# Score banks in units of three, one ring for the probabilities, and numerators divided in halves

## The chip, the cores and the metric

The kernel runs on one core of one Trainium2 chip. The metric is the device time of one execution in microseconds (us). A core has a matrix engine (PE, which writes only to the accumulator memory PSUM), a vector engine (DVE), an activation engine (ACT), a general engine (POOL) and a queue engine (SP) that issues transfers. PSUM has 8 banks per partition, and a bank holds 512 fp32 values. Each engine works through its own instructions in program order and waits for the others through semaphores.

## The reference, cut to what matters

For x of 2048 tokens by 640 (32 heads of 20), the output is `g * A + (1 - g) * B`, with a gate g per token. A is a linear attention with softmax features. B, the part that the change touches, splits the tokens into four segments of 512 and runs, for each head,

```
logits = q @ k.T * scale + mask          # causal within the segment
a_dot  = softmax(logits) @ v
a_mem  = (phi(q) @ M) / (phi(q) @ z + 1e-6)
o      = sig(beta) * a_mem + (1 - sig(beta)) * a_dot
M     += phi(k).T @ v ;  z += sum(phi(k))    # carried to the next segment
```

with `phi(t) = t + 1 if t > 0 else exp(t)`. All heads' o, joined, are multiplied by `wo`.

## The kernel before, in words

The kernel first does all of A and the projections that B's first segment needs (to about 146 us of the profile). Everything the change touches is the second half, "stage B" (L580 to L902), whose order on every engine is the program's order (`manual_schedule`).

Work goes by steps: a step is one segment s and one group g of four heads, so there are 4 x 8 = 32. Keys and queries stand transposed, four heads of 32 rows each. For a step the scores (keys by queries) of key chunk c are computed only for queries from chunk c on: 512, 384, 256 and 128 columns. A bank holds, for one head i, chunk 0 of a step, or chunks 1 and 3 of a step, or chunk 2 of two steps. So two steps fill 20 banks.

`emit_scores` (L613) is a unit of work: two banks, for the heads i0 and i0 + 1. PE makes their scores with matmuls of 32 rows, placed on the row group of their head (L618), and ACT makes exp of both banks into a tile PT (L622). After the second unit of a kind, POOL zeroes the triangles above the diagonal (L630). A pair of steps is ten units, n = 0 to 9.

Between the units PE is given other work, by hand:

- `emit_pv` (L666) multiplies probabilities with v: 40 matmuls of 21 columns for a step (L674), into `nda`. For step a of a pair it is cut into query chunks 0 to 2 (24 matmuls, after unit 9) and chunk 3 (16 matmuls, after unit 0 of the next pair). For step b these come after the units 3 and 4.
- `emit_mem` (L677) adds the memory's part, 4 matmuls (L681), and the next memory's increment, 4 matmuls (L686).
- `emit_epi` (L690) divides, on DVE: reciprocal (L695), weight (L697), one product over both numerators of 640 columns (L707; in segment 0 one of 320, L703), and the memory's increment (L712). POOL adds the halves into oB (L709).
- A half item is a projection of 128 tokens for the next segment, 320 columns wide: 5 matmuls (L505), then a DVE cast (L515). An output half is 5 matmuls (last segment's rows, in segment 0) or 10 (L743), then a DVE cast (L749). `gaps_of` (L790) says after which unit each comes; in most gaps there is one.
- `emit_eq` (L718) and `emit_phiq` (L723) make phi(q) with one ACT and two DVE instructions per step. `turn_keys` (L759) does the same for keys of the next segment (L524, L764, L528).

The PSUM banks of stage B: `bst` two buffers of two banks (scores), `bnd` one buffer of two banks (`nda`), `bps` two buffers of one bank (projections and outputs). A buffer is free for PE when everything that read its last tile is done (`reuse_waits="tile"`).

The tail (L843 to L902) finishes the last two steps, transposes oB on PE with copies on ACT (L858, L859), multiplies with wo (L863), adds the part of A on DVE (L870) and sends the rows out.

Of the kernel before, what the change touches and what calls it, by code (L numbers as in the profile page):

```python
# [15 lines left out]
def kernel(  # L16
# [563 lines left out]
    with ExitStack() as bctx:  # L580
# [7 lines left out]
        bpt = bctx.enter_context(tc.tile_pool(name="bpt", bufs=2))  # L588
# [4 lines left out]
        bps = bctx.enter_context(tc.tile_pool(name="bps", bufs=2, space=bass.MemoryType.PSUM,  # L593
                                              reuse_waits="tile"))
        oBs, ogs = {}, {}
        GP = 4 * (DH + 1)

        class Step:
            def __init__(self, k):
                self.s, self.g = divmod(k, G)  # L600
                self.PT = {}
                self.phiq = None
                if self.g == 0:
                    oBs[self.s] = bw.tile([P, 4, D], BF16, name="oB")
                    og = Eqf[:, 2 * G * L + 2 * L + (self.s % 2) * L:2 * G * L + 2 * L + (self.s % 2 + 1) * L]
                    og = og.bitcast(F32).rearrange("p (n j h) -> p n j h", n=2, j=4)
                    om = omgS[:, 4 * self.s:4 * self.s + 4, None].to_broadcast([P, 4, H])
                    nc.gpsimd.tensor_tensor(out=og[:, 0], in0=om, in1=omgh_b[:, None, :].to_broadcast([P, 4, H]),
                                            op=ALU.mult)
                    nc.gpsimd.tensor_copy(out=og[:, 1], in_=om)  # L610
                    ogs[self.s] = og

        def emit_scores(parts, i0, PT):  # L613
            ps = bst.tile([P, 2, L], F32, name="st_ps")
            for step, c, o in parts:
                kT, qT = (t[step.s % 2][:, step.g] for t in (kTs, qTs))
                for i in (i0, i0 + 1):
                    nc.tensor.matmul(ps[:, i - i0, o:o + L - c * P],  # L618
                                     lhsT=kT[32 * i:32 * i + 32, c * P:(c + 1) * P],
                                     rhs=qT[32 * i:32 * i + 32, c * P:L],  # L620
                                     start=True, stop=True, tile_position=(32 * i, 0))
            nc.scalar.activation(out=PT[:, i0:i0 + 2], in_=ps, func=ACT.Exp, scale=SCALE_B)  # L622

        def triangles(PT, at):
            if at == (0, 2):
                parts = [(PT.rearrange("p i (n t) -> p (i n) t", t=256)[:, :, 0:P], 8)]
            else:
                parts = [(PT[:, :, n * P:(n + 1) * P], 4) for n in at]
            for v, n in parts:
                nc.gpsimd.affine_select(out=v, in_=v, pattern=[[0, n], [1, P]], compare_op=ALU.is_ge,  # L630
                                        fill=0.0, base=0, channel_multiplier=-1)

        def units(a, b):
            out = []
            for st in (a, b):
                for n, parts in enumerate((((st, 0, 0),), ((st, 1, 0), (st, 3, 384)))):
                    PT = bpt.tile([P, 4, L], BF16, name=f"PT{n}")
                    for i0 in (0, 2):
                        def unit(parts=parts, i0=i0, PT=PT, n=n):
                            emit_scores(parts, i0, PT)  # L640
                            if i0 == 2:
                                triangles(PT, (0, 3) if n else (0,))
                        out.append(unit)
                    st.PT[0 if n == 0 else 1] = PT
                if st is a:
                    PT = bpt.tile([P, 4, L], BF16, name="PT2")
                    for i0 in (0, 2):
                        def unit(i0=i0, PT=PT):
                            emit_scores(((a, 2, 0), (b, 2, 256)), i0, PT)
                            if i0 == 2:  # L650
                                triangles(PT, (0, 2))
                        out.append(unit)
                    a.PT[2], b.PT[2] = (PT, 0), (PT, 256)
            return out

        def block(st, c):
            if c == 0:
                return st.PT[0]
            if c == 1:
                return st.PT[1][:, :, 0:384]  # L660
            if c == 3:
                return st.PT[1][:, :, 384:512]
            PT, o = st.PT[2]
            return PT[:, :, o:o + 256]

        def emit_pv(st, js):  # L666
            if js[0] == 0:
                st.nda = bnd.tile([P, 2, 512], F32, name="nda")
            nd = st.nda[:, 0, 0:4 * GP].rearrange("p (j i e) -> p j i e", j=4, i=4)
            vB = vBs[st.s % 2]  # L670
            for j in js:
                for i in range(4):
                    for c in range(j + 1):
                        nc.tensor.matmul(nd[:, j, i], lhsT=block(st, c)[:, i, (j - c) * P:(j - c + 1) * P],  # L674
                                         rhs=vB[:, c, 4 * st.g + i, :], start=(c == 0), stop=(c == j))

        def emit_mem(st):  # L677
            g = st.g
            if st.s > 0:
                for j in range(4):  # L680
                    nc.tensor.matmul(st.nda[:, 1, j * GP:(j + 1) * GP], lhsT=st.phiq[:, j * P:(j + 1) * P],  # L681
                                     rhs=Mbd[:, g].rearrange("p i e -> p (i e)"), start=True, stop=True)
            if st.s < NSEG - 1:
                Mz = st.nda[:, 1, 4 * GP:5 * GP].rearrange("p (i e) -> p i e", i=4)
                for c in range(4):
                    nc.tensor.matmul(Mz, lhsT=phiks[st.s % 2][:, c, 4 * g:4 * g + 4, :],  # L686
                                     rhs=vBs[st.s % 2][:, c, 4 * g:4 * g + 4, :],
                                     start=(c == 0), stop=(c == 3))

        def emit_epi(st):  # L690
            s, g = st.s, st.g
            n = 2 if s > 0 else 1
            ndv = st.nda[:, 0:n, 0:4 * GP].rearrange("p n (ji e) -> p n ji e", e=DH + 1)
            rec = bw.tile([P, 2, 16], F32, name="rec")
            nc.vector.reciprocal(out=rec[:, 0:n], in_=ndv[:, :, :, DH])  # L695
            recv = rec[:, 0:n].rearrange("p n (j i) -> p n j i", j=4)
            nc.vector.tensor_tensor(out=recv, in0=recv,  # L697
                                    in1=ogs[s][:, 0:n, :, 4 * g:4 * g + 4],
                                    op=ALU.mult)
            rb = rec[:, 0:n, :, None].to_broadcast([P, n, 16, DH])  # L700
            oview = oBs[s][:, :, g * 80:(g + 1) * 80].rearrange("p j (i d) -> p j i d", d=DH)
            if n == 1:
                nc.vector.tensor_tensor(out=oview, in0=ndv[:, 0, :, 0:DH].rearrange("p (j i) d -> p j i d", j=4),  # L703
                                        in1=rb[:, 0].rearrange("p (j i) d -> p j i d", j=4), op=ALU.mult)
            else:
                td = bw.tile([P, 2, 16, DH], F32, name="td")
                nc.vector.tensor_tensor(out=td, in0=ndv[:, :, :, 0:DH], in1=rb, op=ALU.mult)  # L707
                tdv = td.rearrange("p n (j i) d -> p n j i d", j=4)
                nc.gpsimd.tensor_tensor(out=oview, in0=tdv[:, 0], in1=tdv[:, 1], op=ALU.add)  # L709
            if s < NSEG - 1:  # L710
                mtmp = bw.tile([P, 4, DH + 1], F32, name="mtmp")
                nc.vector.tensor_tensor(  # L712
                    out=mtmp, in0=st.nda[:, 1, 4 * GP:5 * GP].rearrange("p (i e) -> p i e", i=4),
                    in1=CM[:, g, :, :], op=ALU.mult)
# [3 lines left out]
        def emit_eq(st):  # L718
            eq = Eqf[:, 2 * G * L + (st.g % 2) * L:2 * G * L + (st.g % 2 + 1) * L]
            nc.scalar.activation(out=eq, in_=qTs[st.s % 2][:, st.g], func=ACT.Exp)  # L720
            return eq

        def emit_phiq(st, eq):  # L723
            nc.vector.tensor_scalar_min(out=eq, in0=eq, scalar1=1.0)
            st.phiq = bw.tile([P, L], BF16, name="phiq", bufs=3)
            nc.vector.scalar_tensor_tensor(out=st.phiq, in0=qTs[st.s % 2][:, st.g], scalar=0.0, in1=eq,
                                           op0=ALU.max, op1=ALU.add)
# [6 lines left out]
        oTs, rows = {}, {}  # L734

        def emit_out_half(ch, half):
# [13 lines left out]
            if half == 1 and not early:  # L750
                nc.sync.dma_start(out=out2[ch * P:(ch + 1) * P, :], in_=rows[ch])

        clock = [0]
        due = {}

        def defer(n, fn):
            due.setdefault(clock[0] + n, []).append(fn)

        def turn_keys(sc):  # L759
            emit_turn("k", sc, kTs[(sc // 4) % 2])  # L760
            if sc < NCH - 4:
                def feature():
                    ek = emit_ek(bw, sc)
                    nc.vector.tensor_scalar_min(out=ek, in0=ek, scalar1=1.0)  # L764
                    defer(2, lambda: emit_phik(sc, ek))
                defer(2, feature)
# [10 lines left out]
        def half_items(s, order):  # L777
            return [half_item(part, 4 * s + c, half) for part, c in order for half in range(2)]

        CHUNKED = [(part, c) for c in range(4) for part in "kqv"]  # L780
        FIRST_SEG = [(part, c) for c in range(4) for part in "kq"]
# [151 lines left out]
```

## Time and profile before

| what | value |
|---|---|
| median of 3 runs | 367.07 us (363.47 to 370.16) |
| the profiled execution's own time | 369.4 us |
| its span, first to last instruction | 367.3 us |
| mean granted PE clock | 0.963 |
| PE busy | 337.1 us (92%) |
| ACT busy | 265.1 us (72%) |
| DVE busy | 231.0 us (63%) |
| POOL busy | 205.3 us (56%) |
| first to last exp of stage B | 146.0 to 349.0 us |

The profile counts an instruction as busy from its start to its end. Matmuls are pipelined, so that PE's rows overlap; what an instruction costs PE is read from its start to the next one's start. The granted clock is the share of full speed at which PE was allowed to run.

### The profile page before, as it was taken

What the parts mean: (1) busy time and instruction counts of PE and PEld (TensorE: products, weight loads), DVE (VectorE), ACT (ScalarE), POOL (GpSimd) and SP (SyncE); (2) the same over time, 40 slices, a digit from 0 to 9 for tenths busy, and PEclk for the clock granted to TensorE, in tenths of its full rate; (3) what the DMA queues carried; (4) which work ended last, traced back from release to release, by engine and by line L of the source; (5) the groups of instructions that cost most, each with busy time, mean ns of one, the idle gap of its engine ahead of it and who ended that gap; (6) DMA issues with size and microseconds to landing.
All of it is one profiled execution on the core that took longest, in us unless ns stands there. A gap on an engine that the chain in (4) does not pass through costs nothing.

```text
span 367.3 us, 9701 instructions
## 1 busy us (share of the span) xinstructions
PE 337.1 (92%) x4025; PEld 223.7 (61%) x4025; DVE 231.0 (63%) x469; ACT 265.1 (72%) x342; POOL 205.3 (56%) x283
## 2 busy tenths in 40 slices
PE   7999999899789998898989989889999999999974
PEld 6788888854367775455444455555565655665652
DVE  3466976598778895454353576777667665656533
ACT  4888978058444556987797788778889788898911
POOL 8177598103168778464454466576567456545530
PEclk9999999999899999999995799999999999999969
DMA  8749988980037778422311334213432351130002
GB/s 240 229 88 184 107 109 111 222 297 0 2 16 130 117 112 130 76 42 48 59 31 30 75 39 77 48 33 51 90 59 43 64 85 36 40 74 36 20 20 72
DMA packets 68806, 30.68 MB, mean 84 GB/s; under 512 B 54554, under 2 KB 68762, under 8 KB 68762
## 3 DMA queue, kind: packets, MB, share of 16 engines
q1 hardware_dynamic: 67898, 29.24, 42.0%
q10 hardware_dynamic: 864, 0.82, 0.8%
q8 instruction: 31, 0.51, 0.6%
q14 instruction: 13, 0.11, 0.1%
HBM read 9.21 MB, written 2.62 MB: 32 GB/s over the span
## 4 chain that ended last, share of the span: by engine, by line
PE 65%; ACT 12%; DVE 10%; DMA 6%; issue 5%; POOL 1%; SPq 1%; ACTq 0%; DVEq 0%
PE proj L505 13%; PE st_ps L618 10%; PE o_ps L743 9%; ACT PT L622 9%; PE nda L674 8%; PE pk L213 6%; PE pv L213 6%; PE pq L264 5%; DVE tt L453 2%; DMA Z<-Z 2%; DMA x_nat<-in_A_x_dram 2%; PE num L409 2%; DVE zz L250 2%; DVE rr L431 1%; DMA Z<-EkSn 1%
## 5 line engine op out<-in xcount | busy, mean ns | idle before, releaser
L622 ACT ACTIVATE PT<-st_ps 128x1024 bf16<-128x1024 f32 x160 | 155.6, 1028 | 33.7 <-PE st_ps L618 22.4
L630 POOL TENSOR_SCALAR_AFFINE_SELECT PT<-PT 128x512 bf16<-128x512 bf16 (+1 forms) x112 | 79.4, 726 | 51.0 <-ACT PT L622 50.9
L505 PEld LDWEIGHTS <-xT 128*128 128x128 bf16 x480 | 42.1, 100 | 26.5 <-issue 13.3
L225 POOL TENSOR_TENSOR EkSn<-Ek,krec 128x1280 bf16<-128x1280 bf16 x16 | 37.6, 2360 | 17.6 <-DVE krec L224 15.8
L674 PEld LDWEIGHTS <-PT 128*128 128x128 bf16 x1280 | 36.9, 96 | 15.4 <-issue 12.9
L674 PE MATMUL nda<-vB,PT 128*128 128x21 bf16 x1280 | 42.4, 174 | 1.9 <-DVE td L707 1.7
L213 PEld LDWEIGHTS <-xT 128*128 128x128 bf16 x320 | 35.3, 113 | 7.0 <-ACT xT L191 0.2
L618 PE MATMUL st_ps<-Z 32*128 32x512 bf16 (+3 forms) x256 | 30.2, 302 | 7.6 <-ACT PT L622 5.7
L709 POOL TENSOR_TENSOR oB<-td 128x320 bf16<-128x320 f32 x24 | 20.7, 862 | 23.8 <-DVE td L707 23.8
L618 PE MATMUL st_ps<-Eq 32*128 32x512 bf16 (+3 forms) x256 | 30.1, 314 | 2.9 <-ACT PT L622 2.5
L515 DVE CAST Z<-proj 128x320 bf16<-128x320 f32 x48 | 23.3, 486 | 14.9 <-PE proj L505 14.3
L221 DVE TENSOR_REDUCE ksum<-Ek 128x64 f32<-128x1280 bf16 x16 | 23.6, 1478 | 12.4 <-ACT Ek L217 12.4
L743 PE MATMUL o_ps<-WkA,oTA 128*128 128x320 bf16 x160 | 27.5, 303 | 3.0 <-DVE Z L515 3.0
L269 ACT ACTIVATE Eq<-pq 128x1024 bf16<-128x1024 f32 x20 | 19.4, 1021 | 14.7 <-PE pq L264 14.7
L453 DVE TENSOR_TENSOR tt<-num,rr 128x640 f32<-128x640 f32 x32 | 25.2, 814 | 6.7 <-PE num L409 5.2
L505 PE MATMUL proj<-WqB,xT 128*128 128x320 bf16 x160 | 29.2, 316 | 0.0
L554 POOL TENSOR_TENSOR oA<-tt 128x640 bf16<-128x640 f32 x16 | 24.7, 1548 | 7.6 <-DVE tt L453 6.8
L505 PE MATMUL proj<-WkB,xT 128*128 128x320 bf16 x160 | 28.5, 311 | 0.0
L505 PE MATMUL proj<-WvB,xT 128*128 128x320 bf16 x160 | 27.5, 305 | 0.0
L217 ACT ACTIVATE Ek<-pk 128x640 bf16<-128x640 f32 x32 | 20.8, 701 | 7.7 <-PE pk L213 5.3
L409 PEld LDWEIGHTS <-Eq 128*128 128x128 bf16 x384 | 20.3, 97 | 9.3 <-issue 6.9
L213 PE MATMUL pv<-WvA,xT 128*128 128x321 bf16 x160 | 24.6, 300 | 0.0
(135 smaller groups left out, 540.1 us busy)
## 6 DMA issues: line engine op xcount, KB each, us to landing
Z<-EkSn SPq DMA_DIRECT2D x32, 160.0 KB, 4.9
x_nat<-in_A_x_dram SPq DMA_DIRECT2D x8, 320.0 KB, 6.4
out_dram<-orow SPq DMA_DIRECT2D x12, 160.0 KB, 1.8
WvA<-in_A_wqkv_dram SPq DMA_DIRECT2D x2, 400.0 KB, 6.1
wnat_q<-in_A_wqkv_dram SPq DMA_DIRECT2D x1, 800.0 KB
WkB<-in_B_wk_dram SPq DMA_DIRECT2D x1, 800.0 KB, 7.2
WqB<-in_B_wq_dram SPq DMA_DIRECT2D x1, 800.0 KB, 9.0
WvB<-in_B_wv_dram SPq DMA_DIRECT2D x1, 800.0 KB, 10.6
```

What stands on the lines that cost most here:

```text
L213: nc.tensor.matmul(ps[:, bk, 0:n], lhsT=xTk[:, c, sc // 4, sc % 4], rhs=rhs, start=(c == 0), stop=(c == KC - 1))
L221: nc.vector.tensor_reduce(out=ksum, in_=Ek.rearrange("p s (h f) -> p (s h) f", f=DH), axis=AX.X, op=ALU.add)
L225: nc.gpsimd.tensor_tensor(out=EkSn[:, sc].rearrange("p s (h f) -> p (s h) f", f=DH), in0=Ek.rearrange("p s (h f) -> p (s h) f", f=DH), in1 ...
L409: nc.tensor.matmul(ps(bk, lo, hi), lhsT=Eqs[qb, j][:, sgn, qc * P:(qc + 1) * P], rhs=kvx[:, sgn, j, lo - h0:hi - h0, :].rearrange("p h e - ...
L453: nc.vector.tensor_tensor(out=tt[:, sgn].rearrange("p (b h) d -> p b h d", b=2), in0=ps, in1=csb, op=ALU.mult)
L505: nc.tensor.matmul(ps, lhsT=xT[:, cc, sc * P:(sc + 1) * P], rhs=W[:, cc, half * 320:(half + 1) * 320], start=(cc == 0), stop=(cc == KC - 1))
L554: nc.gpsimd.tensor_tensor(out=oA.rearrange("p (h d) -> p h d", d=DH), in0=tt[:, 0], in1=tt[:, 1], op=ALU.add)
L618: nc.tensor.matmul(ps[:, i - i0, o:o + L - c * P], lhsT=kT[32 * i:32 * i + 32, c * P:(c + 1) * P], rhs=qT[32 * i:32 * i + 32, c * P:L], st ...
L622: nc.scalar.activation(out=PT[:, i0:i0 + 2], in_=ps, func=ACT.Exp, scale=SCALE_B)
L630: nc.gpsimd.affine_select(out=v, in_=v, pattern=[[0, n], [1, P]], compare_op=ALU.is_ge, fill=0.0, base=0, channel_multiplier=-1)
L674: nc.tensor.matmul(nd[:, j, i], lhsT=block(st, c)[:, i, (j - c) * P:(j - c + 1) * P], rhs=vB[:, c, 4 * st.g + i, :], start=(c == 0), stop= ...
L743: nc.tensor.matmul(ps, lhsT=oT[:, k5], rhs=W[:, k5, hs], start=(n == 0 and k5 == 0), stop=(n == len(srcs) - 1 and k5 == KC - 1))
```

## The change

- **Units of three banks.** The 20 banks of a pair of steps become one stream over all steps, 320 banks, cut into 107 units of three (the last has two). PE fills the three banks of a unit, ACT makes exp of all three with one instruction. A unit may run across two kinds of bank. `bst` has two buffers of three banks.
- **The ring.** The probabilities go to one tile of 24 banks, used in turn. The triangles of four banks are zeroed when the fourth is done, as before.
- **Half steps.** `emit_pv` takes a step in two halves of two query chunks: h = 0 has 12 matmuls, h = 1 has 28, each with 2 matmuls of the memory (and h = 1 with the increment). Each half uses one bank, X; `bnd` has one buffer of one bank. Each half is divided right behind: reciprocal, weight, product of 2 x 160 columns.
- **One bank for projections and outputs**: `bps` has one buffer.
- **Dealing.** Items are laid out over a segment and dealt to the units so that the planned cost (0.7 for a half item, 1.38 for an output half, 0.45 and 1.05 for the halves of a step) is spread evenly. In a unit come: the scores, the first item if any, the half step if any, further items. Half steps of step k come in the first and second unit after its last bank (k even) or the second and third (k odd). phi(q) is moved to the end of a unit's work.
- **Outputs**: segments 1, 2, 3 take 4, 4 and 16 output halves (before 3, 5 and 16).
- **Tail.** The first 512 columns of oB are transposed by four transfers in place of PE and ACT. The part of A enters by a matmul with the identity, and the results leave PSUM by copies on DVE and ACT in turn, each followed by a transfer of its half rows.

```diff
-        bpt = bctx.enter_context(tc.tile_pool(name="bpt", bufs=2))
+        bpt = bctx.enter_context(tc.tile_pool(name="bpt", bufs=1))
...
-        bps = bctx.enter_context(tc.tile_pool(name="bps", bufs=2, space=bass.MemoryType.PSUM,
+        bps = bctx.enter_context(tc.tile_pool(name="bps", bufs=1, space=bass.MemoryType.PSUM,
...
+        UB = 3
+        RING = 24
+        ring = bpt.tile([P, RING, L], BF16, name="PT")
...
+        def emit_unit(u):
+            banks = list(range(UB * u, min(UB * u + UB, 10 * NST)))
+            ps = bst.tile([P, UB, L], F32, name="st_ps")
+            todo = [(n, bank(b)) for n, b in enumerate(banks)]
+            for turn in range(2):
+                for n, (kind, i, parts) in todo:
+                    if turn < len(parts):
+                        st, c, o = parts[turn]
+                        kT, qT = (t[st.s % 2][:, st.g] for t in (kTs, qTs))
+                        nc.tensor.matmul(ps[:, n, o:o + L - c * P], ...
+            r0 = banks[0] % RING
+            nc.scalar.activation(out=ring[:, r0:r0 + len(banks)], in_=ps[:, 0:len(banks)],
+                                 func=ACT.Exp, scale=SCALE_B)
...
+        def emit_pv(st, h):
+            s, g = st.s, st.g
+            X = bnd.tile([P, 512], F32, name="X")
+            W2 = 2 * GP
+            nd = X[:, 0:W2].rearrange("p (j i e) -> p j i e", j=2, i=4)
...
+            rec = bw.tile([P, 2, 2, 4], F32, name="rec")
+            nc.vector.reciprocal(out=rec[:, 0:n], in_=v[:, :, :, :, DH])
+            nc.vector.tensor_tensor(out=rec[:, 0:n], in0=rec[:, 0:n],
+                                    in1=ogs[s][:, 0:n, 2 * h:2 * h + 2, 4 * g:4 * g + 4], op=ALU.mult)
...
+                nc.vector.tensor_tensor(out=st.td[:, :, 8 * h:8 * h + 8], in0=v8, in1=rb, op=ALU.mult)
...
+            late = 2 if k % 2 else 1
+            for h in range(2):
+                pv_at.setdefault(min(st_done + late + h, NU + 3), []).append((k, h))
...
+            load = {u: sum(1.05 if h else 0.45 for _, h in pv_at.get(u, ())) for u in us}
+            items = items_of(s)
+            total = sum(load.values()) + sum(c for _, c, _ in items)
+            cum = 0.0
+            for n, u in enumerate(us):
+                cum += load[u]
+                while items and (cum + items[0][1] / 2 <= total * (n + 1) / len(us) or u == us[-1]):
+                    plan[u].append(items[0][2])
+                    cum += items.pop(0)[1]
...
+        for u in range(NU):
+            now[0] = u
+            emit_unit(u)
+            work = plan[u]
+            for fn in work[0:1]:
+                fn()
+            for k, h in pv_at.get(u, ()):
+                emit_pv(step(k), h)
+            for fn in work[1:]:
+                fn()
+            for k in eq_at.get(u, ()):
+                defer(1, emit_eq(step(k)))
...
+                for n in range(4):
+                    nc.sync.dma_start_transpose(out=oT4[:, n, 0:KC - 1, :], in_=oB[:, n, 0:(KC - 1) * P])
+            emit_pv(step(k), h)
```

## The prediction

> **What bounds the kernel now.** I read the page first, for the engines' shares and the granted clock.
>
> ```profile
> PE 337.1 (92%) x4025; PEld 223.7 (61%) x4025; DVE 231.0 (63%) x469; ACT 265.1 (72%) x342; POOL 205.3 (56%) x283
> ...
> PEclk9999999999899999999995799999999999999969
> ```
>
> PE is the busiest, and its clock drops twice. The change touches only stage B, so next came the busy times by segment (four segments, then the tail):
>
> ```profile
> 146.00:194.10 48.10, 41.81 (x553) 23.59 (x554) 21.52 (x56) 40.20 (x44) 24.75 (x41) 0.96 0.27 51
> 194.10:250.90 56.80, 53.44 (x660) 29.44 (x659) 37.40 (x83) 45.20 (x53) 32.69 (x53) 0.89 0.29 53
> 250.90:301.40 50.50, 50.50 (x685) 30.05 (x682) 34.22 (x77) 43.17 (x48) 31.34 (x54) 1.00 0.38 66
> 301.40:349.00 47.60, 45.05 (x651) 28.46 (x648) 26.78 (x58) 42.16 (x48) 27.20 (x42) 1.00 0.15 40
> 349.00:367.30 18.30, 11.08 (x111) 7.50 (x107) 6.07 (x13) 2.85 (x6) 2.95 (x4) 0.81 0.14 46
> ```
>
> The first number behind the length is PE. It sits idle 6.3 + 3.4 + 0 + 2.5 = 12.2 of 203.0 us: stage B is PE's. The clock, in stretches of 3.4 us, the step in which it changes here:
>
> ```profile
> 169.40:172.80 3.40, 2.25 (x40) 1.38 (x38) 2.32 (x7) 3.40 (x5) 0.85 (x2) 1.00 0.02 2
> 172.80:176.20 3.40, 3.40 (x33) 1.76 (x31) 1.11 (x3) 0.94 (x2) 2.01 (x4) 0.50 0.00 0
> ...
> 189.80:193.20 3.40, 2.55 (x41) 1.42 (x38) 0.54 (x2) 3.40 (x4) 1.59 (x2) 1.00 0.42 80
> 193.20:196.70 3.50, 3.50 (x33) 1.52 (x31) 1.40 (x5) 1.99 (x3) 2.77 (x7) 0.51 0.00 0
> ...
> 203.50:206.90 3.40, 3.40 (x14) 1.24 (x13) 1.41 (x3) 2.36 (x3) 2.26 (x4) 0.50 0.04 9
> 206.90:210.30 3.40, 3.40 (x66) 2.24 (x65) 1.90 (x5) 2.61 (x4) 1.16 (x3) 1.00 0.85 165
> ```
>
> Each drop to 0.5 follows a thin stretch. Count columns by 0.43 ns (an item's 5 x 320 take 0.69 us, below), 32-row matmuls as a quarter. Before 193.2 that is 5 x 320 + 24 x 21 + 3072 / 4 = 2872 columns, 1.23 us, 0.36 of the stretch; before 172.8, 0.37. No stretch of stage B with 0.40 or more is followed by a drop. At half clock, stretches of 0.34, 0.32 and 0.38 are followed by more of it, 0.39 and 0.41 by full clock. The 17.1 us at half clock cost 8.5. So stage B is 203.0 = 12.2 idle + 8.5 clock + 182.3 of PE's work.
>
> The timeline gives the prices:
>
> ```profile
> 252.18 0.39 PE L618 MATMUL st_ps<-Z 32*128 32x384 bf16 x4
> ...
> 252.51 0.85 PE L505 MATMUL proj<-WkB,xT 128*128 128x320 bf16 x5
> ...
> 253.29 0.39 PE L618 MATMUL st_ps<-Z 32*128 32x384 bf16 x4
> ...
> 260.44 0.85 PE L505 MATMUL proj<-WvB,xT 128*128 128x320 bf16 x5
> ...
> 261.33 0.49 DVE L515 CAST vB<-proj 128x320 bf16<-128x320 f32 x1 [0.61 <-PE proj L505]
> ```
>
> Scores hold PE 0.33 (252.18 to 252.51). The item behind them takes 0.78 to the next scores, against 0.69 where another item follows (314.08 to 314.77), so 0.09 belongs to the switch: a unit costs 0.42. An item's bank is free again 0.85 (its end) + 0.04 + 0.49 (cast) + 0.06 (217.56 + 0.48 = 218.04, PE starts 218.10) = 1.44 after its start; PE is done issuing at 0.69. The next item can start 0.75 after that.
>
> Two buffers hide this now. Where casts stand behind a division, even two do not, in segment 1:
>
> ```profile
> PE o_ps L743 <- DVE Z L515: 3.0, 3, 1.0
> ```
>
> **The change, part by part.**
>
> Three-bank units: 160 become 107, 53 fewer at 0.42, -22.3 us, as PE is the bound. No row shows three row groups at once. Two take 0.39 us for 32x384 with 32x128 each, a single row 0.384 for 512 columns, so neighbours run side by side, and I take 0.42 for three. The far bound is a serial third, 512 x 0.43 = 0.22 more, +23.5 us over 107; below 0.42 nothing speaks for.
>
> By the Trainium skill ("TensorE: Matmul & The Clock Gate", Part 3, "Measured speedup vs the span model"), four such tiles run 3.07 times as fast as one after another, 1.30 times a single one's 0.22: an estimate of 0.07 more a unit, 7 us in all, and the sum would be 394.
>
> Exp: 1024 columns start 0.904 to 0.921 apart, 512 (L720) 0.52; for 1536 about 1.32. A segment is 27 x 1.32 + 8 x 0.52 + 4 x 0.6 = 42 us of ACT, under PE's time below: nothing. ACT's cover would count only if PE fell to 1.5 us a unit. The triangles are the same in number and size, POOL 25 to 33 us a segment: nothing. The ring's slots come round after 8 units, their last reader is at most 7 units on: nothing.
>
> One bank for projections: I dealt the items by the plan's formula. The time between one item's end and the next decides. Two items in a unit with nothing between stall PE 0.75 (6, 6, 5 and 0 times in the four segments), with half step 0 (0.4) between 0.35 (0, 1, 1, 0). An item, then only scores, then an item: 0.75 - 0.42 = 0.33 (11, 10, 10, 6). Sum by segment: 8.1, 8.2, 7.4, 2.0.
>
> One bank X: the second half step waits for the first one's division. A full step's reciprocal is 0.357, its product 0.825; half of it has the shapes of segment 0's rows, 0.256, 0.20 and 0.49 (202.15 to 203.14). With 0.15 for the matmuls' end, 0.04 and 0.06, X is free 1.24 after the first half; scores (0.42) alone between leave 0.82, scores and an item 0.15. In segment 0, with one numerator (0.21 + 0.19 + 0.32 by the slope of these rows), 0.6 and nothing. Alone 7, 5, 4 and 7 times, with item 0, 3, 4 and 1: 4.2, 4.6, 3.9, 5.9.
>
> Together 44.2 us of stalls. DVE itself has 8 x 0.45 us a segment more to do (two starts instead of one); where a key feature (L764 0.33, L528 0.82 to 1.07) or phi(q) (0.28 + 0.69) stands ahead of a cast, PE waits longer: I take 8 x 0.4 = 3. Bounds of all stalls: 24 (if half find cover) and 60 (if a third more collide).
>
> A walk through units 67 to 78 with these prices gives 27.4 us, 6.6 of it stall: 2.28 us a unit against 12.3 / 6.67 = 1.85 for three banks now (pairs of steps start 250.85, 263.16, 275.47).
>
> The clock: PE does the same full-array columns in more time. Where two units hold only half steps (11-12, 21-22, 84-85, 91-92, 101-102), 6 x 512 / 4 + 40 x 21 + 336 columns, 0.83 us, stand in 2.7 to 3.0 us: 0.28 to 0.30, well under the 0.37 that preceded a drop. Once at half clock, segment 0 runs about 0.31 and segment 3 0.35, under the 0.39 that ended one, so it lasts some stretches. Half clock costs less here, as it runs in the stalls' time: about 1 us per 3.4 us. I take 14 such stretches, 14 us; bounds 0 and 50 (most of stage B).
>
> By the Trainium skill ("TensorE: Matmul & The Clock Gate", "Why this matters for your kernels"), only PE gaps over some 3 us bring the clock down; PE's longest gap before 193.2 is 0.52 us, so the row decides against that rule.
>
> Transposes for the next segment: the last query half is dealt 3 units before segment 1 (now 4 shorter ones), with 3.1 us to landing: 0 to 2 us, with some ACT waits I take 2. On SP nothing else moves far: the oB transposes come 4 to 7 units into a segment, behind its last steps.
>
> Tail: PE's transposes and four ACT copies (0.59 each) go; four transfers come, 1.3 us apart on SP (x2 in 2.52 us) and 2.6 to landing, under the last half steps and the adds. Copies on two engines replace 3.5 us of DVE sums. The last bank still waits for X. I take -2; bounds -6 (the ACT waits, 7.4 us, mostly gone) and +4 (transfers late).
>
> **Sum.** Stage B: 182.3 - 22.3 + 47 + 2 + 14 = 223, +20. With the tail 369.4 + 20 - 2 = 387. This is against the profiled execution's own 369.4 (span 367.3 and 2.1 around it), which stands 2.3 over the median of the runs.
>
> **The rivals.**
>
> - The stalls find cover, and PE's saving shows: faster. By segment the larger of PE (busy, less the clock's loss, less 13.3 units at 0.42) and ACT is 38, 42, 45 and 40, stage B 165 us, with a quarter of the stalls left 177: 369.4 - 203 - 2 + 165 to 177, 329 to 341. For it: PE's items average one a unit. Against: program order and one buffer. It decides below 205 - 162 = 43 us of stalls and clock together; I count 61.
> - Half the stalls covered: 160 + 24 + 2 + 14 = 200, 364.
> - No drop of the clock: the stalls are each under 1 us, and gaps of 0.96 and 1.03 us now (217.1, 230.6) bring none. 387 - 14 = 373. The skill's rule above would have it so; the trace so far does not.
> - The clock stays down for half of stage B or more, or the third row group is serial: 410 to 425.
>
> **How the numbers follow.** Forecast 0.48 (own range 374 to 402); cover 0.15; half cover 0.10; no drop 0.10; worse 0.17. A measurement of this kernel tells about 2% from no change. Faster (under 362) 0.16, same 0.22, slower (over 377) 0.62. The range: of the cover case most is left out below, and the worst end above, 355 to 418.
>
> **What would show it.** L618 should fall to 107 units of about 0.39 us; a unit of 0.6 would show the serial third. PE's waits should name the casts (L515, L749) for some 20 to 25 us and the division (td) for some 18; if both are under 10, the cover rival is right. PEclk should show drops in segments 0 and 3. ACT idle per unit should grow, not shrink. Wrong altogether would be a stage B under 200 us.

## The result and the profile after

The changed kernel takes 400.44 us (median of 4 runs, 397.00 to 401.37) where the kernel before takes 368.12: a ratio of 1.095, 95% interval 1.080 to 1.109. It is slower, as forecast, and 13 us slower than the forecast 387, at the upper end of the forecast's own range of 374 to 402. The profiled execution took 401.37 us with a span of 399.5. Over all its runs the kernel before took 361.52 to 374.54 us at mean granted clocks from 0.995 down to 0.943, so the clock's losses below are those of one execution of each kernel.

The page, lines 1 and 2, of the kernel after:

```profile
PE 335.5 (84%) x4014; PEld 226.0 (57%) x4017; DVE 251.7 (63%) x563; ACT 262.6 (66%) x289; POOL 203.8 (51%) x283
...
PEclk9999999999999999996569996989699989899899
```

PE is as busy in microseconds as before (337.1), in a longer span: its share falls from 92% to 84%. The clock drops in all four segments of stage B, not twice.

The busy times by segment (cut at the first exp of units 27, 54 and 80), and then the tail:

```profile
145.80:201.40 55.60, 43.70 (x558) 24.76 (x558) 28.09 (x81) 40.88 (x33) 24.86 (x44) 0.84 0.27 45
201.40:268.30 66.90, 51.74 (x671) 30.80 (x671) 43.32 (x108) 45.02 (x40) 31.39 (x52) 0.88 0.26 47
268.30:328.40 60.10, 50.28 (x673) 30.81 (x672) 38.57 (x99) 41.26 (x34) 30.81 (x52) 0.91 0.31 53
328.40:383.80 55.40, 45.73 (x639) 28.75 (x637) 32.44 (x82) 41.70 (x35) 28.58 (x43) 0.94 0.13 34
383.80:399.50 15.70, 9.10 (x99) 6.09 (x96) 4.21 (x11) 2.29 (x5) 2.55 (x4) 0.97 0.34 87
```

Stage B grows from 203.0 to 238.0 us, in every segment, and PE's idle time in it from 12.2 to 46.5. The tail falls from 18.3 to 15.7. DVE is 65% busy in its worst segment, ACT 75%: no engine has taken PE's place as the bound. What PE waits for, in stage B alone (us in total, times, longest):

```profile
PE X L688 <- DVE td L716: 17.9, 18, 2.2
PE proj L505 <- DVE Z L515: 13.0, 22, 2.6
PE X L688 <- DVE oB L710: 4.8, 8, 0.9
PE proj L505 <- DVE vB L515: 2.7, 7, 0.6
PE proj L505 <- DVE oTA L762: 2.5, 4, 0.9
PE o_ps L756 <- DVE Z L515: 1.9, 7, 0.3
PE o_ps L756 <- DVE orow L762: 1.0, 4, 0.3
```

The two banks that have become single take nearly all of it: PE waits 17.9 + 4.8 = 22.7 us for divisions before it can fill X again, and 22.4 us for casts before it can fill the bank of projections and outputs (the five lines here and two small ones). The wait for a score bank is gone; it was the largest of stage B before:

```profile
PE st_ps L618 <- ACT PT L622: 8.3, 20, 1.0
```

ACT's exp, in the page's groups, now idles 66.0 us behind scores that come late, where it idled 22.4 us (before, then after):

```profile
L622 ACT ACTIVATE PT<-st_ps 128x1024 bf16<-128x1024 f32 x160 | 155.6, 1028 | 33.7 <-PE st_ps L618 22.4
L653 ACT ACTIVATE PT<-st_ps 128x1536 bf16<-128x1536 f32 (+1 forms) x107 | 152.5, 1445 | 70.1 <-PE st_ps L648 66.0
```

The longest waits hold more than one bank's turnaround. The timeline of the kernel after, at the end of segment 1:

```profile
259.92 0.47 PE L688 MATMUL X<-vB,PT 128*128 128x21 bf16 x12
...
260.24 0.23 PE L694 MATMUL X<-Mbd,phiq 128*128 128x84 bf16 x2
...
260.43 0.69 DVE L733 SCALAR_TENSOR_TENSOR phiq<-Eq 128x512 bf16<-128x512 bf16 x1
260.46 2.27 POOL L664 TENSOR_SCALAR_AFFINE_SELECT PT<-PT 128x1024 bf16<-128x1024 bf16 x2
...
261.03 1.21 DVE L781 TENSOR_SCALAR ek<-ek 128x640 bf16<-128x640 bf16 x1
261.42 0.84 PE L756 MATMUL o_ps<-WvA,oT 128*128 128x320 bf16 x5
262.28 1.13 DVE L528 SCALAR_TENSOR_TENSOR Z<-Z,ek 128x640 bf16<-128x640 bf16 x1
263.33 0.25 DVE L703 RECIPROCAL rec<-X 128x16 f32<-128x16 f32 x1
...
263.89 0.49 DVE L716 TENSOR_TENSOR td<-X,rec 128x320 f32<-128x320 f32 x1
...
264.44 0.87 PE L688 MATMUL X<-vB,PT 128*128 128x21 bf16 x28 [2.18 <-DVE td L716]
```

The first half's sums are done at 260.47. DVE comes to them at 263.33, since phi(q) and a key feature stand ahead in its queue, and PE stands still for 2.18 us. The two instructions of the key feature took 1.21 and 1.13 us here; with no POOL instruction beside them they take 0.32 and 0.82 in this trace, so 1.2 us of the delay came from their being slow (see the last section). The stretch of the clock that holds this wait (columns behind the length: PE busy, weight loads, DVE, ACT, POOL, granted clock):

```profile
258.50:261.90 3.40, 3.08 (x37) 1.89 (x37) 2.43 (x5) 3.40 (x4) 3.33 (x5) 1.00 0.41 77
261.90:265.30 3.40, 1.22 (x35) 0.89 (x34) 2.71 (x6) 0.98 (x1) 0.84 (x2) 1.00 0.00 0
265.30:268.80 3.50, 3.46 (x23) 1.44 (x21) 1.57 (x5) 2.51 (x3) 2.00 (x6) 0.51 0.13 47
```

Full-array columns, counted as in the prediction, fill 0.17 of the middle stretch, and the next runs at half clock: a wait is paid for twice. Stage B has 15 such stretches (51.2 us).

To set this against the sum, I split stage B by the matmul records of each trace. The price of a matmul is the mean time from its start to the next one's start where PE neither idles nor runs at half clock, by kind and by the kind that follows. What a matmul takes above its price is a wait where PE then stood idle, and the clock's loss in a half-clock stretch; the rest is work. The split depends on how finely the kinds are told apart: pricing by line alone, or by line and shape, moves each term by up to 3 us (work before 178.4 or 181.3, after 165.5 or 163.4).

| stage B, us | length | work | waits | clock |
|---|---|---|---|---|
| before, as the prediction split it | 203.0 | 182.3 | 12.2 | 8.5 |
| before, by the records | 203.0 | 179.6 | 16.8 | 6.5 |
| after, predicted | 223 | 160.0 | 49 | 14 |
| after, by the records | 238.0 | 165.1 | 56.4 | 16.3 |

### The profile page after: what moved, and what is told of

It reads as the page before. It is cut to its first block, busy times and chain, and to the rows that moved or that the text cites. A ratio compares the mean times of both kernels' runs of the same rounds, so it can differ in the third digit from the quotient of the medians.

```text
span 399.5 us, 9768 instructions
## 1 busy us (share of the span) xinstructions
PE 335.5 (84%) x4014; PEld 226.0 (57%) x4017; DVE 251.7 (63%) x563; ACT 262.6 (66%) x289; POOL 203.8 (51%) x283
## 3 DMA queue, kind: packets, MB, share of 16 engines
q1 hardware_dynamic: 70362, 29.85, 39.6%
## 4 chain that ended last, share of the span: by engine, by line
PE 54%; DVE 31%; DMA 5%; issue 5%; POOL 1%; ACT 1%; SPq 0%; DVEq 0%; ACTq 0%
PE proj L505 13%; PE o_ps L756 10%; PE X L688 7%; PE pk L213 5%; PE pv L213 5%; DVE Z L515 4%; PE pq L264 4%; DVE td L716 4%; DVE rec L704 3%; PE st_ps L648 3%; DVE orow L762 2%; DVE rec L703 2%; DVE tt L453 2%; DVE phiq L733 2%; DMA x_nat<-in_A_x_dram 2%
## 5 line engine op out<-in xcount | busy, mean ns | idle before, releaser
L653 ACT ACTIVATE PT<-st_ps 128x1536 bf16<-128x1536 f32 (+1 forms) x107 | 152.5, 1445 | 70.1 <-PE st_ps L648 66.0
L664 POOL TENSOR_SCALAR_AFFINE_SELECT PT<-PT 128x512 bf16<-128x512 bf16 (+1 forms) x112 | 78.0, 711 | 86.9 <-ACT PT L653 86.3
L505 PEld LDWEIGHTS <-xT 128*128 128x128 bf16 x480 | 45.7, 102 | 49.0 <-issue 33.7
L688 PE MATMUL X<-vB,PT 128*128 128x21 bf16 x1280 | 42.9, 174 | 24.7 <-DVE td L716 19.1
L688 PEld LDWEIGHTS <-PT 128*128 128x128 bf16 x1280 | 39.5, 97 | 38.1 <-DVE td L716 25.2
L213 PEld LDWEIGHTS <-xT 128*128 128x128 bf16 x320 | 35.4, 113 | 6.7
L505 PE MATMUL proj<-WkB,xT 128*128 128x320 bf16 x160 | 30.5, 326 | 7.5 <-DVE Z L515 4.1
L703 DVE RECIPROCAL rec<-X 128x16 f32<-128x16 f32 (+1 forms) x64 | 15.4, 240 | 30.1 <-PE X L699 20.5
L756 PE MATMUL o_ps<-WkA,oTA 128*128 128x320 bf16 x160 | 30.4, 325 | 4.0 <-DVE Z L515 1.9
L221 DVE TENSOR_REDUCE ksum<-Ek 128x64 f32<-128x1280 bf16 x16 | 23.6, 1478 | 12.5 <-ACT Ek L217 12.5
L716 DVE TENSOR_TENSOR td<-X,rec 128x320 f32<-128x320 f32 x48 | 23.6, 491 | 3.0
L648 PE MATMUL st_ps<-Z 32*128 32x512 bf16 (+3 forms) x256 | 23.8, 330 | 1.0 <-DMA Z<-Z 1.0
```

Source lines behind the costliest of these rows:

```text
L213: nc.tensor.matmul(ps[:, bk, 0:n], lhsT=xTk[:, c, sc // 4, sc % 4], rhs=rhs, start=(c == 0), stop=(c == KC - 1))
L505: nc.tensor.matmul(ps, lhsT=xT[:, cc, sc * P:(sc + 1) * P], rhs=W[:, cc, half * 320:(half + 1) * 320], start=(cc == 0), stop=(cc == KC - 1))
L648: nc.tensor.matmul(ps[:, n, o:o + L - c * P], lhsT=kT[32 * i:32 * i + 32, c * P:(c + 1) * P], rhs=qT[32 * i:32 * i + 32, c * P:L], start=T ...
L653: nc.scalar.activation(out=ring[:, r0:r0 + len(banks)], in_=ps[:, 0:len(banks)], func=ACT.Exp, scale=SCALE_B)
L664: nc.gpsimd.affine_select(out=v, in_=v, pattern=[[0, m], [1, P]], compare_op=ALU.is_ge, fill=0.0, base=0, channel_multiplier=-1)
L688: nc.tensor.matmul(nd[:, jj, i], lhsT=block(st, c, i, j), rhs=vB[:, c, 4 * g + i, :], start=(c == 0), stop=(c == j))
```

## The experiments

My theory: stage B pays for two single PSUM banks, whose turnaround PE waits out, then for DVE's queue in front of casts and divisions, then for the clock that falls in these waits. Rivals: the wider units themselves are slow (a serial third row group, a longer exp), the clock is the main loss and not the waits, or DVE's larger load is the bound. All ratios are to the kernel before, run beside each kernel.

**One bank in the kernel before.** Everything as before, but projections and outputs have one bank:

```diff
-        bps = bctx.enter_context(tc.tile_pool(name="bps", bufs=2, space=bass.MemoryType.PSUM,
+        bps = bctx.enter_context(tc.tile_pool(name="bps", bufs=1, space=bass.MemoryType.PSUM,
...
-        late = {(2, half): bps.tile([P, 320], F32, name="o_ps", tag="ps1") for half in range(2)}
+        bp2 = bctx.enter_context(tc.tile_pool(name="bp2", bufs=1, space=bass.MemoryType.PSUM))
+        late = {(2, 0): bps.tile([P, 320], F32, name="o_ps", tag="ps1"),
+                (2, 1): bp2.tile([P, 320], F32, name="o_ps")}
```

> The kernel before (368 us) with one bank instead of two for projections and outputs (the freed bank serves only one tile of the tail); all else stays. If one bank costs PE the eviction's turnaround: 0.33 us at each item with scores alone ahead of it, and waits behind the division on DVE, 20 to 30 us of idle PE more and some half clock: 385 to 400. If two banks were more than it needs: 367 to 372.

Measured: 407.25 us, ratio 1.113 (1.105 to 1.122), with units of two, whole divisions and the old dealing. By the records, waits grow from 16.8 to 46.0 us and the clock's loss from 6.5 to 15.6; work stays (178.9). Its waits in stage B begin so:

```profile
PE proj L505 <- DVE Z L515: 14.0, 17, 1.8
PE st_ps L618 <- ACT PT L622: 5.8, 11, 1.2
PE proj L505 <- DVE orow L749: 4.7, 8, 0.6
```

The time lies above the expected 385 to 400: one lost bank does as much harm as the whole change. The run took nothing from the change's units or its DVE load, so neither is needed to explain such a loss.

**Two banks in turn, shared.** The change, but X and the items rotate over the same two banks:

```diff
-        bnd = bctx.enter_context(tc.tile_pool(name="bnd", bufs=1, space=bass.MemoryType.PSUM,
+        bnd = bctx.enter_context(tc.tile_pool(name="bnd", bufs=2, space=bass.MemoryType.PSUM,
                                               reuse_waits="tile"))
-        bps = bctx.enter_context(tc.tile_pool(name="bps", bufs=1, space=bass.MemoryType.PSUM,
-                                              reuse_waits="tile"))
+        bps = bnd
...
-            X = bnd.tile([P, 512], F32, name="X")
+            X = bnd.tile([P, 512], F32, name="X", tag="ps1")
```

> The changed kernel (400 us) with its two single PSUM banks, one for half steps and one for items, put into one rotation of two buffers that both use in turn. Work, order and bank count stay. If PE's stalls come from each kind of tile having only one bank: a tile then waits only for the one two places back, the 46 us of idle PE in stage B fall to 10 to 15 (what is queued on DVE), and with them most of the 51 us at half clock; stage B falls from 238 to about 180, the time to 335 to 355. If DVE's load, with the division cut in two, is the cause: the waits move to the next tile, 385 to 400. If the clock falls by itself: idle PE falls, the half clock stays near 50 us, 370 to 380.

Measured: 362.82 us, ratio 0.990 (0.983 to 0.997). Not one bank more, no instruction less, and 38 us are gone: waits 26.6, clock 7.1, work unchanged (166.2). PE's waits in stage B now begin so:

```profile
PE X L687 <- POOL PT L663: 4.7, 7, 1.7
PE X L687 <- DVE td L715: 4.0, 5, 1.7
PE proj L505 <- DVE Z L515: 3.1, 4, 1.1
```

The gain is smaller than expected (335 to 355): PE still idles 21.6 us, part of it for POOL's triangles. But the wide units, the halves and DVE's load are all still there, so none of them by itself is the loss.

**Units of two banks, with two banks each for X and the items.** The change with `UB = 2`, `bnd` and `bps` at two buffers (and the places of the tail's sums fitted to it):

```diff
-        bnd = bctx.enter_context(tc.tile_pool(name="bnd", bufs=1, space=bass.MemoryType.PSUM,
+        bnd = bctx.enter_context(tc.tile_pool(name="bnd", bufs=2, space=bass.MemoryType.PSUM,
...
-        bps = bctx.enter_context(tc.tile_pool(name="bps", bufs=1, space=bass.MemoryType.PSUM,
+        bps = bctx.enter_context(tc.tile_pool(name="bps", bufs=2, space=bass.MemoryType.PSUM,
...
-        UB = 3
+        UB = 2
```

> The changed kernel with units of two banks (160 of them), which leaves two banks for half steps and two for items; half steps, ring, dealing and tail stay as changed. If the single banks made the loss, and not the halves, the dealing or the tail: no turnaround stalls, PE's work back at the old 182 us in stage B, 10 us of waits, little half clock: 362 to 378. If the halves' additional DVE work or the planned dealing cost by themselves: 385 to 400.

Measured: 366.42 us (10 runs), ratio 1.004 (0.998 to 1.010): no difference from the kernel before. The stream, the ring, the halves, the dealing and the tail together come out even; what the change loses lies in what the third score bank displaces.

**What the wider unit is worth.** The shared rotation again, with `UB = 2`:

```diff
-        bps = bctx.enter_context(tc.tile_pool(name="bps", bufs=1, space=bass.MemoryType.PSUM,
...
+        bps = bnd
...
-        UB = 3
+        UB = 2
```

> Units of two banks with the shared rotation of two buffers of e1_shared (363 us); two PSUM banks stay unused until the tail. Against e1_shared only the size of the units differs, so this measures what 53 units fewer are worth. If a unit costs PE 0.42 us and PE is the bound: 15 to 22 us more than e1_shared, 376 to 385. If ACT or DVE's queue is what e1_shared waits for: 360 to 368.

Measured: 375.93 us, ratio 1.029 (1.018 to 1.041), 13 us above the kernel with units of three, just under the 15 to 22 expected. By the records work is 185.8 against 166.2: 53 units hold 19.6 us of PE, 0.37 each, where I had 0.42. The units of three give some 8 us of that back in longer waits (26.6 against 18.5), but they do bring a gain.

**One item a unit.** The change with its items laid out by number alone, so that two rarely meet in one unit:

```diff
-            load = {u: sum(1.05 if h else 0.45 for _, h in pv_at.get(u, ())) for u in us}
...
-            total = sum(load.values()) + sum(c for _, c, _ in items)
-            cum = 0.0
-            for n, u in enumerate(us):
-                cum += load[u]
-                while items and (cum + items[0][1] / 2 <= total * (n + 1) / len(us) or u == us[-1]):
-                    plan[u].append(items[0][2])
-                    cum += items.pop(0)[1]
+            for n, it in enumerate(items):
+                plan[us[min(n * len(us) // len(items), len(us) - 1)]].append(it[2])
```

> The changed kernel with its items laid one to a unit (by number, not by planned cost); banks and the rest stay. If the stalls are those of two items in one unit and of a second half step with no item ahead of it: the 17 pairs at 0.75 us and most of the 23 lone second halves at 0.8 us go, more pairs with scores alone between (0.33) come, PE's idle time falls from 46 to about 25 us and the half clock to 20 to 30 us: 365 to 378. If DVE's queue sets the stalls wherever the items stand: 392 to 402.

Measured: 375.35 us, ratio 1.025 (1.018 to 1.032). 25 us less with the same single banks: waits 38.9, clock 6.2. While the banks are single, dealing by planned cost, blind to who holds the bank, makes up most of the 32 us that the change lost; with two banks each (366 us, above) the same dealing cost nothing.

**Keeping PE's columns up.** Two matmuls of 512 columns into the first score bank in each unit that has no item, work that adds nothing. There are 30 such units (the trace has 60 of these matmuls), and not 24 as the expectation says:

```diff
+            for _ in range(0 if plan[u] else 2):
+                nc.tensor.matmul(ps[:, 0, :], lhsT=ident_b, rhs=xT[:, 0, 0:L], start=True, stop=True)
```

> The changed kernel with two matmuls of 512 columns more, in each of the 24 units without an item, into the first bank of the unit ahead of its scores, which then overwrite it (0.43 us a unit, 10 us of PE work in all, that adds nothing to the result). These units stand ahead of a wait for the division. If the clock drops when a 3.4 us stretch has under 0.39 of its columns filled: the half clock falls from 51 to 15 to 30 us, the added work hides in the stalls, and the time falls by 5 to 15 us, to 385 to 395. If the half clock costs nothing because it runs in the stalls' time: 400 to 404. If it follows idle time and not columns: 400 to 410 with the half clock near 50 us.

Measured: 399.72 us, ratio 1.091 (1.081 to 1.101): the time of the change itself. The expected 5 to 15 us did not come. But half clock fell from 51.2 to 23.9 us, so filling the thin stretches keeps the clock up; as the filler also shortened waits, columns and idle time are not told apart by this run alone. By the records it gave 7.8 us of clock and filled 8.5 us of waits, and cost 12.4 us of work (30 units at 0.43 are 12.9). The clock is a real loss, but a small one beside the waits: 7.8 us for 27.3 us at half clock, 0.29 for each.

**Features kept away from the halves.** DVE's feature work is put off while the next unit has a half step, at most two units:

```diff
+        pend = []
...
-            for fn in due.pop(u, []):
-                fn()
+            pend += [(u, fn) for fn in due.pop(u, [])]
+            while pend and (not pv_at.get(u + 1) or u - pend[0][0] >= 2):
+                pend.pop(0)[1]()
+                if not pend or u - pend[0][0] < 2:
+                    break
```

> The changed kernel (400 us), with the feature work on DVE (the clamps and sums of phi(q) and phi(k)) taken one per unit, and not at the end of a unit that a half step follows unless it is two units late. Banks, units and dealing stay. My prediction gave DVE's queue 3 us of waits; if the 13 us that it was short are features standing ahead of a division or a cast (waits of 2.2 and 2.6 us in the trace): PE's idle time falls from 46 to about 35 us, 386 to 394. If the shortfall is elsewhere (PE's work, the clock): 398 to 402.

Measured: 422.30 us (420.46 to 429.76), where the kernel before took 361.52 to 370.51 beside it. I had expected a gain; it lost 22 us more. Its trace shows why: waits for the division fell from 17.9 to 12.9 us, and those for casts doubled (22.4 to 46.8), since put-off features now come in a row:

```profile
238.08 0.39 PE L648 MATMUL st_ps<-Eq 32*128 32x512 bf16 x5
...
238.58 0.28 DVE L731 TENSOR_SCALAR Eq<-Eq 128x512 bf16<-128x512 bf16 x1
...
238.89 1.23 DVE L733 SCALAR_TENSOR_TENSOR phiq<-Eq 128x512 bf16<-128x512 bf16 x1
...
240.05 0.48 DVE L781 TENSOR_SCALAR ek<-ek 128x640 bf16<-128x640 bf16 x1
...
240.56 0.83 DVE L528 SCALAR_TENSOR_TENSOR Z<-Z,ek 128x640 bf16<-128x640 bf16 x1
...
241.30 0.48 DVE L515 CAST Z<-proj 128x320 bf16<-128x320 f32 x1
...
241.84 0.42 PE L756 MATMUL o_ps<-WkA,oTA 128*128 128x320 bf16 x1 [3.37 <-DVE Z L515]
```

The cast stands behind 2.7 us of features, and PE waits 3.37. The place of features in DVE's queue costs PE directly, but moving them this way only chose which bank is kept waiting. How much they cost had to be measured another way.

**The features taken out.** In both kernels ACT writes the bare exponential in place of phi; DVE's part is gone. The changed kernel's edit (that of the kernel before is the same, in its lines):

```diff
-            eq = Eqf[:, 2 * G * L + st.odd * L:2 * G * L + (st.odd + 1) * L]
-            nc.scalar.activation(out=eq, in_=qTs[st.s % 2][:, st.g], func=ACT.Exp)
...
+            st.phiq = bw.tile([P, L], BF16, name="phiq", bufs=3)
+            nc.scalar.activation(out=st.phiq, in_=qTs[st.s % 2][:, st.g], func=ACT.Exp)
+            return lambda: None
...
-                    ek = emit_ek(bw, sc)
...
+                    nc.scalar.activation(out=phiks[(sc // 4) % 2][:, sc % 4, :, 0:DH],
+                                         in_=stages["k"][sc % 2][:, :, 0:DH], func=ACT.Exp)
```

> The changed kernel without VectorE's part of the features of stage B: phi(q) and the later segments' phi(k) are the bare exponential, written by ScalarE in the place where it wrote it already; the minimum and the maximum-and-add (L731, L733, L781, L528: 39.8 us of VectorE in stage B) are left out, so the memory's part is of other features than the reference's. Everything else stays, order and PSUM banks too. Theory (the waits beyond the turnaround of one bank come from feature work that stands in VectorE's queue ahead of casts and divisions, a term taken as 3 us and held to be about 13 now): PE's waits on casts and division fall from about 46 to 33 us, two to four of the stretches at half clock go, and the time falls by 10 to 17 us, to 383 to 390. Rival (the turnaround of a bank alone sets the waits, and VectorE has time for the features while PE works): at most 4 us less, 396 to 400.

> The same cut in the kernel before (36.2 us of VectorE in stage B, L724, L726, L764, L528): phi(q) and the later phi(k) are the bare exponential, of other features than the reference's. Its PE idles 12.2 us in stage B, so both theories allow little: 362 to 368, at most 6 us below the kernel before. If it falls by as much as the changed kernel does, the features cost both kernels the same and are not what the change made dearer.

Measured: the changed kernel 385.82 us, ratio 1.052 (1.045 to 1.059); the kernel before 363.37, ratio 0.985 (0.980 to 0.991). Against the change's own 1.095, leaving the features out takes 4.2 points, 15.6 us, and from the kernel before 1.5 points, 5.3. So the features cost the change about 10 us more than the kernel before (4 to 17 by the intervals, added as squares). By the records of the changed kernel, waits fall from 56.4 to 49.5 and the clock's loss from 16.3 to 9.1. What is left are PE's waits for divisions and casts, and the long cast waits are gone:

```profile
PE X L688 <- DVE td L716: 14.8, 16, 1.8
PE proj L505 <- DVE Z L515: 10.4, 24, 1.0
PE X L688 <- DVE oB L710: 4.5, 8, 0.7
```

The cast waits' longest is 1.0 where it was 2.6. Most of the waits, 49.5 us, are there without any feature; the shared rotation, which keeps the features, brings them to 26.6. So the single banks are the larger part.

**Towards a better kernel.** The shared rotation with one item a unit, and the half steps a unit later for the even steps:

```diff
-        bps = bctx.enter_context(tc.tile_pool(name="bps", bufs=1, space=bass.MemoryType.PSUM,
+        bps = bnd
...
-            late = 2 if k % 2 else 1
+            late = 2
...
+            for n, it in enumerate(items):
+                plan[us[min(n * len(us) // len(items), len(us) - 1)]].append(it[2])
```

> e1_shared (363 us) with one item to a unit, and the half steps of the even steps one unit later, so that POOL's triangles are done ahead of them (e1_shared waits 5.6 us for these). If what is left there is waits that such an order avoids (21.6 us of idle PE in stage B): idle 8 to 12 us and half clock under 10 us, 345 to 355. If DVE's load sets these waits: 358 to 365.

Measured: 357.88 us, ratio 0.980 (0.970 to 0.991): waits 23.6, clock 5.6. That misses the expected 345 to 355 and stands at the edge of the rival's 358 to 365; PE still idles 19.1 us where 8 to 12 were expected. Whether DVE's load is behind it, the next run decides.

Then units of three and two banks in turn (5 score banks in place of 6), and the bank that this frees as a third one of the shared rotation; 128 units, a ring of 20 banks:

```diff
-        bst = bctx.enter_context(tc.tile_pool(name="bst", bufs=2, space=bass.MemoryType.PSUM,
+        bst = bctx.enter_context(tc.tile_pool(name="bst", bufs=1, space=bass.MemoryType.PSUM,
...
-        bnd = bctx.enter_context(tc.tile_pool(name="bnd", bufs=1, space=bass.MemoryType.PSUM,
+        bnd = bctx.enter_context(tc.tile_pool(name="bnd", bufs=3, space=bass.MemoryType.PSUM,
...
-        RING = 24
+        unit_of = lambda b: 2 * (b // 5) + (b % 5 >= 3)
+        first_of = lambda u: 5 * (u // 2) + 3 * (u % 2)
+        RING = 20
...
+            banks = list(range(first_of(u), first_of(u + 1)))
+            ps = bst.tile([P, len(banks), L], F32, name="st_ps", tag=f"st{u % 2}")
```

> As e7_shared_one_each, but units of three and two banks in turn (128 units, five banks of PSUM, a ring of 20 banks), and three banks in the shared rotation. PE has 21 units more at 0.42 us, 9 us, and a third buffer. If the third buffer takes the waits that are left: 345 to 355, about as e7_shared_one_each. If two shared buffers were enough: 8 to 10 us over e7_shared_one_each.

Measured: 349.04 us, ratio 0.954 (0.943 to 0.966). It beats both kernels: its slowest run, 350.01, is below the fastest of the kernel before beside it, 362.63. Its page, and stage B in one row:

```profile
PE 321.5 (92%) x4014; PEld 222.6 (64%) x4017; DVE 252.9 (73%) x563; ACT 260.8 (75%) x310; POOL 207.6 (60%) x283
```

```profile
146.00:330.00 184.00, 175.80 (x2538) 110.53 (x2539) 142.50 (x367) 166.65 (x160) 119.84 (x188) 0.99 0.33 59
```

DVE has the same work as in the change (251.7 there) and stage B is 54 us shorter: DVE's load is no bound. By the records, work is 171.4 (21 units more than in the kernel above, +5.9), waits 10.8, clock 1.3. A score bank given up for a bank of the rotation pays.

The last kernel is this one with the rule on features that failed above:

```diff
-            for fn in due.pop(u, []):
-                fn()
+            pend += [(u, fn) for fn in due.pop(u, [])]
+            while pend and (not pv_at.get(u + 1) or u - pend[0][0] >= 2):
...
```

> e8_three_two (349 us) with the same rule for the feature work. With three shared buffers little waits for DVE (idle PE 8 us, 6 of it for ACT): 346 to 350. If DVE's queue still decides there: under 345.

Measured: 348.93 us (347.67 to 350.83), no change. The rule cost 22 us with single banks and nothing with three in rotation, where PE has other banks to go on with while a cast or division is late.

## Why the prediction was right, and where it was off

- **The mechanism held, the size did not.** PE's waits name what the prediction said: casts 22.4 us (20 to 25 forecast), divisions 22.7 (about 18). Stage B with one bank in the old kernel, and the change with a shared rotation, show from both sides that the banks are the cause. The cover rival is out: waits and clock came to 73 us, far beyond the 43 at which it decided. But the range was wide (355 to 418), and stage B grew by 35.0 us where 20 were forecast.
- **The unit of three costs what the pair costs.** The timeline of the kernel after:

```profile
335.98 0.39 PE L648 MATMUL st_ps<-Eq 32*128 32x512 bf16 x3
336.31 0.46 PE L688 MATMUL X<-vB,PT 128*128 128x21 bf16 x12
```

  Three row groups hold PE for 0.33, as two did. The serial third is out. The estimate of 7 us more, worked out from the Trainium skill ("TensorE: Matmul & The Clock Gate", Part 3, "Measured speedup vs the span model"), does not show either.
- **Work, the term that failed most: -22.3 forecast, -14.5 by the records** (179.6 to 165.1), 7.8 off, and 4 to 9 off with the other pricings. The step "53 fewer at 0.42" was mis-sized: the two shared rotations, which differ in the unit's size and deal by the same rule, show 0.37 each, 19.6. I also took 0.33 + 0.09 for every unit, while some units before had no item between them and so no switch. And the stream, the halves and the dealing cost PE some 4 to 8 us, by the pricing, that I put at nothing: units of two in the changed order hold 185.8 of work, the kernel before 179.6. Which of the three costs it was not tried.
- **The clock: +5.5 forecast (14 for 8.5), +9.8 measured (16.3 for 6.5).** 14 stretches were forecast, 15 came, each at about the 1 us taken (16.3 / 15 = 1.09); the prediction took both figures without working them out, so that the nearness is in part luck. The error is in the kernel before: its 17.1 us at half clock cost 6.5, not half of them, as part of it ran where PE waited anyway. The Trainium skill ("TensorE: Matmul & The Clock Gate", "Why this matters for your kernels") warns of PE gaps over some 3 us, a window of idle that brings the clock down. No wait of the kernel after in stage B is longer than 2.6 us, and it has 15 half-clock stretches: here shorter waits did it. The rule read from the rows held: every stretch after which the clock fell was filled to 0.39 or less.
- **Waits: +36.8 forecast (49 for 12.2), +39.6 measured (56.4 for 16.8).** Counted as the prediction counted, by the waits that name the two banks, 45.1 us came for 47 forecast (44.2 of turnaround and 3 of DVE's queue). That nearness is luck in part: with the features gone these waits are 39.4, so the turnaround was put too high and DVE's queue too low. The 3 us taken for the queue were too few: 6.9 by the records without the features, and 7.2 of clock that went with them.
- **The tail**: -2 forecast, -2.6 measured.
- The three differences, 7.8 + 4.3 + 2.8, are the 15 us by which stage B grew more than forecast (+35.0 for +20). In this split they all lie on one side. With its margin of some 3 us a term, the shortfall is sure for work and for the sum, and not for the waits: PE's plain idle time grew by 34.3 us (12.2 to 46.5), less than the 36.8 forecast.
- **Open**: how the loss divides between X and the items' bank was not tried in the changed kernel. What is said of it here rests on the names of the waits, 22.7 and 22.4 us.

## What to carry to other kernels

Before a PSUM bank is given to a wider unit, work out the turnaround of the buffer that loses it: here 0.75 us an item beyond PE's own time, with PE in program order, cost more than the 53 units saved. If banks are scarce, let different users rotate over the same ones and deal their work so that no two follow each other: the same eight banks, shared out and dealt in other ways, gave 400, 363 and 349 us. Once a buffer is single, each instruction ahead of its reader in that engine's queue can be on the path, and a wait is paid again where it thins a stretch and the clock falls.

## What the runs showed of the hardware

- **Clock.** Over five kernels (before, after, the shared rotation, one item a unit, three-and-two) stretches of 3.4 us filled with full-array columns to 0.40 or less preceded every drop in stage B, some from 0.37 to 0.41 brought none, and half clock lasted after 0.39 or less and ended after 0.39 to 0.49. In three further kernels (both with units of two, and the one with features kept away) one drop each came after 0.41. The edge is not sharper than 0.37 to 0.41 in the records, some of which can be missing.
- **DVE beside POOL.** The key feature's minimum took 1.21 us at 261.03, while POOL zeroed triangles (260.46 to 262.73), and 0.33 in the mean before. The weight's product took 0.91 at 337.86 beside a triangle that ran from 337.66 to 338.75, and 0.17 at 263.62. In the whole trace of the change this product took 0.17 to 0.18 us in all 36 cases in which no triangle was running when it began. Of the 28 that began beside one, 20 took longer, 0.20 to 0.91, and each of these ended within 0.03 us after a triangle ended. So the trace ties the stretch to the end of POOL's triangle, and a stall behind DVE grows with where POOL's work falls. No run took POOL's triangles away.
- **A wider exp** costs less a column: 1445 ns for 1536 columns against 1028 ns for 1024. Behind each other they start 1.36 apart (three took 4.17 us from 258.72), near the 1.32 forecast.
